# Partial logits transposed and added on VectorE, and three drains of GpSimd, in a retention and mixture-of-experts kernel

## The chip, the cores and the metric

The kernel runs on one core of one Trainium2 chip. The metric is the time of one execution in device microseconds (us), taken as the median of several runs. A core has five engines that work through their own instruction lists in order and wait for each other by semaphores: TensorE (PE, with its weight loads shown apart as PEld), VectorE (DVE), ScalarE (ACT), GpSimd (POOL) and SyncE (SP), which here only issues transfers.

## The reference

Inputs: q, k and v of 8 sequences, 8 heads, 576 positions and 64 numbers a head; 16 experts in 4 groups of 4.

```
scores = q @ k.T / 8                      # per sequence and head
x = (scores * gamma[h] ** (i - j), i >= j) @ v      # 4608 tokens x 512
g = argmax(x @ w_group);  e = argmax(x @ w_expert[g])
weight = softmax(x @ w_group)[g] * softmax(x @ w_expert[g])[e]
out = weight * (relu(x @ w1[g, e]) @ w2[g, e])      # each token by its one expert
```

All of it is float32. A token needs 20 logits: 4 for its group and 16 for the experts.

## The kernel before

The kernel has two stages. In the first (the loop at line 650) 36 tiles of 128 tokens go through the retention: products of k and q into PSUM (`pss`), a mask on VectorE (`sT`), products with v into PSUM (`px`), added products with the running state (`px` again, from `st`), and a multiplication on VectorE that makes the transposed tokens `xT` (line 640). Three tiles form a group, and each group is routed once:

- `logits` (line 351): the 512 numbers of a token lie in 4 chunks of 128. For each chunk one product gives 20 partial logits (padded to 32 rows) for the 384 tokens of the group, and the four chunks land in the four quarters of the 128 partitions of one PSUM tile, `plt`. ScalarE copies it to `lt`.
- `gate` (line 361): three products, one for each tile, of `lt` with the constant 0/1 matrix `sel`, which turns the tile (tokens onto partitions) and adds the four partial sums in one step, into `pl`, 20 numbers for each token and tile. VectorE then takes maxima (`mx`), differences (`df`) and one-hot choices (`oh`, `ob`).
- `weigh` and `places` (lines 403 and 420): the weights `wt`, and by products with triangular and all-ones matrices (`pp`) the row of each token in a table `xs` in HBM, sorted by expert. `xnat` (line 331) turns the tokens back (`pxt`, 4 transposes on TensorE for a tile), scales them (`xt`) and scatters them to `xs` with an indirect transfer of GpSimd.

`gate` of a group runs three tiles after the group's last one, between the scores of that tile and the value products of the tile before it. In the second stage (line 897) the 16 experts are worked through one after another, each in 8 steps of the hidden size, with float32 split into two halves (`wh`, `wl`; `xTh`, `xTl`), which makes three products of each one. GpSimd scatters the finished outputs of expert p - 1 during expert p (`ystore`, line 840), two blocks a step from the second step on, each paced by a one-element copy (`pace`, line 952) that waits for that step's first layer. The last group's `gate` stands in this stage, in the second step of the first expert (line 914).

The order of each engine's list is the order in which the code is written: every instruction is pinned behind the one before it on its engine (line 95). The value products of a tile write the one buffer of `px`, so they wait until VectorE has read the tile before into `xT`. On VectorE that `xT` stands behind the whole of `gate`. Helper calls all go through line 118, so rows of the profile carry that line and are told apart by the tiles' names.

Of the kernel before, what the change touches and what calls it, by code (L numbers as in the profile page):

```python
# [7 lines left out]
F32 = mybir.dt.float32  # L8
# [4 lines left out]
ALU = mybir.AluOpType  # L13
AX = mybir.AxisListType

P = 128
RG = 3
B, H, S, D = 8, 8, 576, 64
N, DM = B * S, H * D
G, EG, F = 4, 4, 1024  # L20
E = G * EG
NP = H // 2
NKC = DM // P
NFC = F // P
# [30 lines left out]
KC_BLK = KC_ROOM + 1  # L55
KC_CAP = KC_BLK + OVB
KC_CAPB = KC_CAP + E
KC_SEL = KC_CAPB + E
KC = KC_SEL + G + E

KC_MASK = KC
KC_GQ = KC_MASK + 2 * P
KC_ALL = KC_GQ + 5 * NP * P
GE = G + E
# [3 lines left out]
def moe_retention(ctx, tc, qk, kv, wgt, w1, w2, c_f, out):  # L68
# [10 lines left out]
    cf = cp.tile([P, KC], F32, name="cf")  # L79
    gk = cf[:, KC_GK : KC_GK + 5 * H].rearrange("p (c h) -> p c h", c=5)  # L80
    ident = cf[:, KC_ID : KC_ID + P]
    eid = cf[:, KC_EID : KC_EID + E]
    sel = cf[:, KC_SEL : KC_SEL + GE]
    rank = cf[:, KC_4 : KC_4 + 4]
    slb = cf[:, KC_SLB : KC_SLB + NB]
    sln = cf[:, KC_SLN : KC_SLN + 3]
# [20 lines left out]
    class Ordered:  # L107
# [15 lines left out]
    pe, dve, act, pool, sp = [  # L123
        Ordered(e_) for e_ in (nc.tensor, nc.vector, nc.scalar, nc.gpsimd, nc.sync)
    ]
# [150 lines left out]
    def ids(p):  # L276

        ii = gp.tile([P, NB], I32, name=f"ii_{p}", tag="ii", bufs=3)
        if natural(p):
            nt = len(ttiles(p))  # L280
            dve.tensor_scalar(
                ii[:, 0:nt], idns[p][:, 0:nt, 0].bitcast(I32), 2, None, ALU.logical_shift_right
            )
            dve.tensor_tensor(ii[:, 0:nt], ii[:, 0:nt], (mi0 if p == 0 else mil)[:, 0:nt], ALU.bitwise_or)
        else:
            nb = nblocks(p)
            dve.tensor_tensor(
                ii[:, 0:nb], xg[p][:, 0:nb, DQ].bitcast(I32), mia[:, p, 0:nb], ALU.bitwise_or
            )
        iis[p] = ii  # L290
# [3 lines left out]
    tiles = []  # L294
    for bp in range(B // 2):
        for j in range(9):
            if j < 8:
                b, c = 2 * bp + j // 4, j % 4
# [26 lines left out]
    sm = ctx.enter_context(tc.tile_pool(name="sm", bufs=2))  # L325
# [34 lines left out]

    def gate(t):

        pl = ps_sm.tile([P, RG, GE], F32, name=f"pl_{t}", tag="sm")
        for x_ in range(RG):
            pe.matmul(pl[:, x_, :], tiles[t]["lt"][:, x_, :], sel, start=True, stop=True)

        def t_(nm, shape, dt=F32):
            return sm.tile([P, RG] + shape, dt, name=f"{nm}_{t}", tag=nm)

        K = G + 1  # L370
        n = RG
        lv = pl.rearrange("p r (k e) -> p r k e", e=4)
        mx = t_("mx", [K])
        dve.tensor_reduce(mx, lv, AX.X, ALU.max)
        df = t_("df", [K, 4])
        dve.tensor_tensor(df, lv, mx.unsqueeze(3).to_broadcast([P, n, K, 4]), ALU.subtract)
        ex = t_("ex", [K, 4])
        act.activation(ex, df, AF.Exp)
        oh = t_("oh", [K, 4])
        dve.scalar_tensor_tensor(  # L380
            oh.rearrange("p r k e -> p (r k) e"), df.rearrange("p r k e -> p (r k) e"), 0.0,
            rank.unsqueeze(1).to_broadcast([P, n * K, 4]), ALU.is_ge, ALU.mult,
        )
        m2 = t_("m2", [K])
        dve.tensor_reduce(m2, oh, AX.X, ALU.max)
        dve.tensor_tensor(
            oh, oh, m2.unsqueeze(3).to_broadcast([P, n, K, 4]), ALU.is_equal
        )
        tiles[t]["rt"] = ex, oh
        ob = obs[-1][:, 1:, :]  # L390
        dve.tensor_tensor(
            ob.rearrange("p r (g e) -> p r g e", g=G), oh[:, :, 1:, :],
            oh[:, :, 0, :].unsqueeze(3).to_broadcast([P, n, G, EG]), ALU.mult,
        )
# [99 lines left out]
    with ExitStack() as ac:  # L494
# [155 lines left out]
        for t in range(NT + 1):  # L650
# [12 lines left out]
            r = t - PICK  # L663
# [233 lines left out]
    for p in range(E):  # L897
        for f in range(NFC):
            pc = p * NPIECE + f // 2
            if p == 0:  # L900
                new = {2: (4, 5), 3: (6,), 5: (7,)}.get(f, ())
            else:
                new = range(pc + 3, pc + 5) if f % 2 == 0 else ()
            for i in new:
                if i not in raws and (i >= len(pieces) or pieces[i][0] in ereg):
                    load_piece(i)
            layer1(p, f)
            if (p, f) == (0, 0):
                logits(NT - 1)
                xnat(NT - 5)  # L910
                pick(1)
            if (p, f) == (0, 1):
                expert_of(1)
                gate(NT - 1)
                xnat(NT - 4)
            if (p, f) == (0, 2):
                places(NT - 1)
                weigh(NT - 1)
                xnat(NT - 3)
            if (p, f) == (0, 3):  # L920
                xnat(NT - 1)
                xload(1)
            if (p, f) == (0, 4):
                for kc in range(NKC):
                    xsplit(0, kc)
            if (p, f) == (0, 6):
                for i in range(3):
                    xturn(1, i, 3)
                for kc in range(NKC):
                    xsplit(1, kc)  # L930
            if 2 * pc + f % 2 + 3 >= WHOLE:
                split(2 * pc + f % 2 + 3)
            if prev is not None:
                layer2(*prev)
                if f == 0:
                    for i in range(NKC if p > 1 else 2):
                        yturn(p - 1, i) if p > 1 else finish(0, i)
            if (p, f) == (0, 2):
                tiles_counted()
                xnat(NT - 2)  # L940
                count_experts()
            if (p, f) in ((0, 4), (0, 5)):
                next(ranks, None)
            if (p, f) == (0, 6):
                expert_of(2)
            if (p, f) == (0, 7):
                next(ranks, None)
            if p > 1 and f > 0:
                for b in range(2 * (f - 1), 2 * f):
                    if b < nblocks(p - 1):  # L950

                        pool.tensor_copy(pace, hts[p, f][0][0:1, 0:1].bitcast(F32))
                    ystore(p - 1, b)
            if f == (4 if p > 0 else 7) and p + 2 <= E:
                xpad(p + 2)
            if f == (5 if p > 0 else 7):
                xload(p + 2)
            if (p, f) == (2, NFC - 3):
                ov = overflow_places(cp)
                ovt = overflow_tables(*ov, mp, ring, cnt, cf, req, dve)  # L960
            if p in (2, 3):
                next(ovt, None) if (p, f) >= (2, NFC - 3) else None
            if f == NFC - 3 and p:
                for i in range(3):
                    xturn(p + 1, i, 3)
            if f == NFC - 2 and p:
                for kc in range(NKC):
                    xsplit(p + 1, kc)
            if f == NFC - 1 and p + 1 < E:
                ids(p + 1)  # L970
            prev = (p, f)
    for pc in range(NPIECE):
        last1(pc)
# [197 lines left out]
def _consts():  # L1171
    import numpy as np

    gamma = 1.0 - 2.0 ** (-5.0 - np.arange(H, dtype=np.float64))
    p = np.arange(P)
    c = np.zeros((P, KC_ALL), np.float32)
    pos = np.stack([ci * P + (p if ci < 4 else p % 64) for ci in range(5)])
    for ci in range(5):
        c[:, KC_GK + ci * H : KC_GK + (ci + 1) * H] = gamma[None, :] ** -pos[ci][:, None].astype(np.float64)
    c[:, KC_ID : KC_ID + P] = np.eye(P)  # L1180

    rel = p[None, :] - p[:, None]
    c[:, KC_MASK : KC_MASK + P] = rel >= 0
    c[:, KC_MASK + P : KC_GQ] = (rel >= 0) & (p[None, :] // 64 == p[:, None] // 64)

    for ci in range(5):
        for o in range(2):
            for s in range(2):
                col = KC_GQ + ((ci * 2 + o) * 2 + s) * P
                for g in range(2):  # L1190
                    c[g * D : g * D + D, col : col + P] = gamma[4 * s + 2 * g + o] ** pos[ci][None, :] / np.sqrt(D)
    c[:, KC_UP : KC_UP + P] = p[:, None] < p[None, :]
    c[:, KC_EID : KC_EID + E] = np.arange(E)

    c[:, KC_ENS : KC_ENS + E] = np.arange(E) * np.where(p < NS // 32 - P, 64, 32)[:, None]
    c[:, KC_SEL : KC_SEL + GE] = p[:, None] % 32 == np.arange(GE)
    c[:, KC_4 : KC_4 + 4] = [4, 3, 2, 1]
    c[:, KC_TRI:KC_SLB] = np.tril(np.ones((E, E))).reshape(-1)
    c[:, KC_BLK:KC_CAP] = np.arange(OVB)
    c[:, KC_CAP : KC_CAP + E] = CAPS  # L1200
    c[:, KC_CAPB : KC_CAPB + E] = -(-np.array(CAPS) // 32) * 32
    c[:, KC_SLB:KC_SLN] = np.arange(NB)[None, :] * 32 + p[:, None] % 32
    c[:, KC_SLN:KC_ROOM] = np.arange(3)[None, :] * P + p[:, None]
    c[:, KC_ROOM] = EARLY - 2 * p
    return c
# [61 lines left out]
```

## Time and profile before

| | |
|---|---|
| median of 3 runs | 620.37 us (620.37 to 621.72) |
| the profiled execution | 622.87 us, span 621.1 us |
| TensorE busy | 598.5 us, 96% of the span |
| VectorE busy | 422.0 us, 68% |
| ScalarE busy | 329.0 us, 53% |
| GpSimd busy | 263.2 us, 42% |
| mean granted TensorE clock | 0.987 |

The span runs from the first instruction to the last, and the execution's own time is 1.8 us longer. Busy shares are means over both stages. The retention fills the first 160 us or so, the experts the rest.

### The profile page before, as it was taken

The page shows a single profiled execution, that of the slowest core. Times are in us where ns is not written, and L with a number is a line of the kernel's source. Part 1 is how long each engine was busy: PE and PEld are TensorE (multiplying, and loading weights), DVE is VectorE, ACT ScalarE, POOL GpSimd, SP SyncE. Part 2 cuts the span into 40 slices and gives each one's busy share as a digit, 9 for nine tenths or more (in the row PEclk, how much of TensorE's full clock was granted, in tenths as well). Part 3 has the DMA queues.
Part 4 walks back from the last instruction along what each step waited for, and adds up shares of the span by engine and source line. Part 5 has one row for each costly group of instructions (what it writes and reads, how often), then busy time and mean ns, then how long its engine had stood idle before and what let it go on. Part 6 is the DMA issues. An engine that isn't in the chain of part 4 may idle for free.

```text
span 621.1 us, 15503 instructions
## 1 busy us (share of the span) xinstructions
PE 598.5 (96%) x5651; PEld 560.4 (90%) x5651; DVE 422.0 (68%) x955; ACT 329.0 (53%) x849; POOL 263.2 (42%) x389
## 2 busy tenths in 40 slices
PE   7899999999999999999999999999999999999990
PEld 7788788888768999999999999999999999999980
DVE  2576666677568576997767685776867768668670
ACT  3777777776255344434535353554545545546460
POOL 0022222223222017494645538185383553743751
PEclk8899999999999999999999999999999999999996
DMA  8998898877883971919375573918649467494800
GB/s 332 417 402 311 327 339 295 302 283 225 272 271 109 309 270 45 321 33 321 103 280 148 221 244 129 322 58 314 204 165 319 114 259 229 151 323 138 338 27 18
DMA packets 63262, 144.22 MB, mean 232 GB/s; under 512 B 9393, under 2 KB 30393, under 8 KB 63184
## 3 DMA queue, kind: packets, MB, share of 16 engines
q1 hardware_dynamic: 53648, 122.65, 56.8%
q0 software_dynamic: 9248, 20.35, 9.1%
q8 instruction: 45, 0.74, 0.5%
q14 instruction: 33, 0.27, 0.1%
q10 hardware_dynamic: 288, 0.22, 0.1%
HBM read 122.85 MB, written 24.88 MB: 238 GB/s over the span
## 4 chain that ended last, share of the span: by engine, by line
PE 88%; DMA 4%; DVE 2%; issue 1%; ACT 1%; POOL 1%; SPq 0%; POOLq 0%; ACTq 0%
PE py L118 33%; PE ph L118 32%; PE px L118 8%; PE pss L118 6%; PE pxt L118 3%; PE pst L118 2%; DMA b<-in_kv 2%; PE plt L118 1%; PE pl L118 1%; DMA xb<-xs 1%; POOL out L118 1%; DMA xs<-xt,sl 1%; PE phn L118 0%; PE pp L118 0%; DVE wl L118 0%
## 5 line engine op out<-in xcount | busy, mean ns | idle before, releaser
L118 POOL DMA_INDIRECT out<-y,ii x152 | 167.8, 1104 | 53.9 <-issue 37.5
L118 DVE TENSOR_TENSOR wl<-r,wh 128x512 fp32r<-128x512 f32 x260 | 167.7, 687 | 6.8 <-ACT xt L118 3.1
L118 ACT ACTIVATE hh<-ph 128x356 fp32r<-128x356 f32 (+16 forms) x128 | 53.8, 420 | 210.3 <-PE ph L118 139.9
L118 PE MATMUL ph<-xTh_m,wh 128*128 128x356 f32 (+15 forms) x488 | 147.5, 302 | 0.8 <-ACT xTh_m L118 0.8
L118 PE MATMUL ph<-xTl_m,wh 128*128 128x356 f32 (+15 forms) x488 | 146.8, 301 | 0.1
L118 ACT CAST wh<-r 128x512 fp32r<-128x512 f32 x260 | 146.9, 617 | 0.0
L118 PE MATMUL ph<-xTh_m,wl 128*128 128x356 f32 (+15 forms) x488 | 146.7, 301 | 0.0
L118 PE MATMUL py<-hh,wh 128*128 128x288 f32 (+17 forms) x480 | 145.0, 302 | 0.0
L118 PE MATMUL py<-hl,wh 128*128 128x356 f32 (+14 forms) x480 | 144.7, 302 | 0.0
L118 PE MATMUL py<-hh,wl 128*128 128x356 f32 (+14 forms) x480 | 144.6, 301 | 0.0
L118 DVE SCALAR_TENSOR_TENSOR hl<-ph,hh 128x356 fp32r<-128x356 f32 (+15 forms) x122 | 56.7, 465 | 103.7 <-ACT hh L118 71.9
L118 PEld LDWEIGHTS ph<-xTh_m,wh 128*128 128x128 f32 x488 | 92.0, 189 | 1.7 <-ACT xTh_m L118 1.2
L118 PEld LDWEIGHTS ph<-xTl_m,wh 128*128 128x128 f32 x488 | 92.1, 189 | 0.9 <-DVE xTl_m L118 0.4
L118 POOL COPY pace<-hh 1x1 f32<-1x1 f32 x140 | 34.6, 247 | 136.1 <-ACT hh L118 133.6
L118 PEld LDWEIGHTS ph<-xTh_m,wl 128*128 128x128 f32 x488 | 92.2, 189 | 0.0
L118 PEld LDWEIGHTS py<-hh,wh 128*128 128x128 f32 x480 | 90.6, 189 | 0.2
L118 POOL DMA_INDIRECT xs<-xt,sl x36 | 35.9, 996 | 129.5 <-ACT xt L118 98.6
L118 PEld LDWEIGHTS py<-hl,wh 128*128 128x128 f32 x480 | 90.4, 188 | 0.2 <-DVE hl L118 0.2
L118 PEld LDWEIGHTS py<-hh,wl 128*128 128x128 f32 x480 | 90.5, 188 | 0.0
L118 ACT ACTIVATE vs<-b,cf 128x64 f32<-128x64 f32 x288 | 72.5, 336 | 10.5 <-DMA b<-in_kv 10.5
L118 DVE TENSOR_TENSOR sT<-pss,masks 128x512 f32<-128x512 f32 x72 | 46.4, 685 | 43.8 <-PE pss L118 38.3
L118 PEld LDWEIGHTS pss<-a 64*128 64x128 f32 x576 | 36.2, 193 | 11.5 <-issue 4.6
(160 smaller groups left out, 630.5 us busy)
## 6 DMA issues: line engine op xcount, KB each, us to landing
r<-in_w SPq DMA_DIRECT2D x138, 512.0 KB
a<-in_qk SPq DMA_DIRECT2D x35, 512.0 KB
b<-in_kv SPq DMA_DIRECT2D x35, 512.0 KB
xb<-xs SPq DMA_DIRECT2D x24, 148.5 KB
xb<-xs SPq DMA_DIRECT2D x20, 165.0 KB
out<-y,ii POOLq DMA_INDIRECT x152
xb<-xs SPq DMA_DIRECT2D x12, 181.5 KB
gq<-c_f SPq DMA_DIRECT2D x5, 256.0 KB
```

Of the source, the lines that this page charges most:

```text
L118: i_ = f(*a, **k)
```

## The change

Three things are edited. In `gate` the three products with `sel` become three transposes on TensorE, each against the identity, which put all 128 rows of partial sums of a tile onto the free axis of `pl` (now 128 numbers for each token and tile instead of 20). A new reduction on VectorE adds the four numbers that belong together, which lie 32 apart, into a tile `lg` in SBUF, and the maxima and differences are taken from `lg`. The constant `sel` is gone, which makes the constants 20 columns narrower. And GpSimd gets a drain instruction, without a semaphore, at the end of the last step of experts p = 5, 10 and 14.

```diff
-    sel = cf[:, KC_SEL : KC_SEL + GE]
...
-        pl = ps_sm.tile([P, RG, GE], F32, name=f"pl_{t}", tag="sm")
+        pl = ps_sm.tile([P, RG, P], F32, name=f"pl_{t}", tag="sm")
         for x_ in range(RG):
-            pe.matmul(pl[:, x_, :], tiles[t]["lt"][:, x_, :], sel, start=True, stop=True)
+            pe.transpose(pl[:, x_, :], tiles[t]["lt"][:, x_, :], ident)
...
-        lv = pl.rearrange("p r (k e) -> p r k e", e=4)
+        lg = t_("lg", [GE])
+        dve.tensor_reduce(
+            lg, pl.rearrange("p r (a g) -> p r g a", a=NKC)[:, :, 0:GE], AX.X, ALU.add
+        )
+        lv = lg.rearrange("p r (k e) -> p r k e", e=4)
         mx = t_("mx", [K])
         dve.tensor_reduce(mx, lv, AX.X, ALU.max)
...
             if f == NFC - 1 and p + 1 < E:
                 ids(p + 1)
+            if f == NFC - 1 and p in (5, 10, 14):
+
+                pool.drain(fusable=False)
```

On VectorE, the fifth `gate` of the program stands before so, between the masks of a tile and the `xT` of the tile before it:

```order
L118 TENSOR_TENSOR sT_1404<-pss_0_1394,masks 128x512
L118 TENSOR_TENSOR sT_1404<-pss_1_1395,masks 128x512
L118 TENSOR_REDUCE mx_1411<-pl_1407 128x15
L118 TENSOR_TENSOR df_1413<-pl_1407,mx_1411 128x60
L118 SCALAR_TENSOR_TENSOR oh_1417<-df_1413,cf 128x60
L118 TENSOR_REDUCE m_14_1419<-oh_1417 128x15
L118 TENSOR_TENSOR oh_1417<-oh_1417,m_14_1419 128x60
L118 TENSOR_TENSOR ob_1267<-oh_1417 128x48
L118 TENSOR_TENSOR xT_1363<-px_1423,gq_115 128x4x128
```

After the change the same place has one reduction more, ahead of the maxima (the listing's line numbers are two lower):

```order
L116 TENSOR_TENSOR sT_1412<-pss_0_1402,masks 128x512
L116 TENSOR_TENSOR sT_1412<-pss_1_1403,masks 128x512
L116 TENSOR_REDUCE lg_1419<-pl_1415 128x60
L116 TENSOR_REDUCE mx_1421<-lg_1419 128x15
L116 TENSOR_TENSOR df_1423<-lg_1419,mx_1421 128x60
L116 SCALAR_TENSOR_TENSOR oh_1427<-df_1423,cf 128x60
L116 TENSOR_REDUCE m_14_1429<-oh_1427 128x15
L116 TENSOR_TENSOR oh_1427<-oh_1427,m_14_1429 128x60
L116 TENSOR_TENSOR ob_1275<-oh_1427 128x48
L116 TENSOR_TENSOR xT_1371<-px_1433,gq_115 128x4x128
```

The `xT` now stands behind seven instructions of the gate instead of six, and `mx` and `df` read `lg` instead of `pl`. This is so in each of the twelve gates.

On TensorE, around the seventh gate, before:

```order
L118 MATMUL pss_1_1867<-a_1383 128x128
L118 MATMUL pl_1879<-cf,lt_1853 128x20 x3
L118 MATMUL px_1895<-sT_1802,vs_1697 64x128 x8
L118 MATMUL pst_1816<-vs_1783,b_1432 64x64 x8
L118 MATMUL pxt_1917<-cf,xT_1363 128x128 x4
```

And after:

```order
L116 MATMUL pss_1_1879<-a_1391 128x128
L116 MATMUL pl_1891<-cf,lt_1865 128x128 x3
L116 MATMUL px_1909<-sT_1814,vs_1709 64x128 x8
L116 MATMUL pst_1828<-vs_1795,b_1442 64x64 x8
L116 MATMUL pxt_1931<-cf,xT_1371 128x128 x4
```

Nothing moves on TensorE. The three instructions on `pl` now have the form of those on `pxt`, which are transposes too. The lists of ScalarE, GpSimd (the drains aside) and SyncE are as before, but for the narrower transfer of the constants.

## Rows read from the trace of the kernel before

**Rows 1.** Busy time by engine in a stretch of either stage; us.

```profile
core 0: us, PE busy (x) PEld busy (x) DVE busy (x) ACT busy (x) POOL busy (x), PEclk, DMA share, GB/s
72.00:84.00 12.00, 12.00 (x199) 9.73 (x191) 7.72 (x21) 9.08 (x31) 3.26 (x5) 1.00 0.88 291
225.00:240.00 15.00, 15.00 (x97) 15.00 (x97) 8.97 (x17) 5.82 (x13) 7.66 (x13) 1.00 0.27 104
```

**Rows 2.** The chain that ended last: start us, us, what.

```profile
78.42 0.78 PE pl L118 x6
80.81 0.59 PE pxt L118 x4
...
182.69 5.17 DMA xb<-xs
```

**Rows 3.** Tile pl: ns min/median/max, first and last start us, forms.

```profile
L118 PEld LDWEIGHTS pl<-cf,lt x72: 186/192/192, 28.8 to 165.5; 128*128 128x128 f32 x72
L118 PE MATMUL pl<-cf,lt x72: 183/266/287, 28.8 to 165.5; 128*128 128x20 f32 x72
```

**Rows 4.** Tile pxt, the same columns.

```profile
L118 PEld LDWEIGHTS pxt<-cf,xT x144: 137/140/224, 34.5 to 174.8; 128*128 128x128 f32 x144
```

**Rows 5.** Timeline of weight loads around the twelfth gate: start us, us, what.

```profile
164.80 0.85 PEld L118 LDWEIGHTS pl<-cf,lt 128*128 128x128 f32 x6
165.49 0.50 PEld L118 LDWEIGHTS pxt<-cf,xT 128*128 128x128 f32 x4
```

**Rows 6.** Reductions on VectorE by form: busy us, mean ns, idle before.

```profile
L118 DVE TENSOR_REDUCE ov_bt<-ov_small 128x49 f32<-128x784 f32 x3 | 2.9, 972 | 0.1
...
L118 DVE TENSOR_REDUCE ov_cape<-ov_b 128x16 f32<-128x256 f32 x1 | 0.6, 603 | 0.0
...
L118 DVE TENSOR_REDUCE rk<-kk 128x16 f32<-128x256 f32 x1 | 0.4, 420 | 0.0
```

**Rows 7.** Timeline of VectorE in the fifth gate, the same columns.

```profile
79.65 0.21 DVE L118 TENSOR_REDUCE mx<-pl 128x15 f32<-128x60 f32 x1
79.89 0.22 DVE L118 TENSOR_TENSOR df<-pl,mx 128x60 f32<-128x60 f32 x1
...
81.03 0.69 DVE L118 TENSOR_TENSOR xT<-px,gq 128x512 f32<-128x512 f32 x1
```

**Rows 8.** The same, the xT behind gates one, four, six, ten and eleven.

```profile
31.47 0.68 DVE L118 TENSOR_TENSOR xT<-px,gq 128x512 f32<-128x512 f32 x1
...
68.56 0.68 DVE L118 TENSOR_TENSOR xT<-px,gq 128x512 f32<-128x512 f32 x1
...
93.53 0.69 DVE L118 TENSOR_TENSOR xT<-px,gq 128x512 f32<-128x512 f32 x1 [0.23 <-PE px L118]
...
144.71 0.68 DVE L118 TENSOR_TENSOR xT<-px,gq 128x512 f32<-128x512 f32 x1
...
156.66 0.68 DVE L118 TENSOR_TENSOR xT<-px,gq 128x512 f32<-128x512 f32 x1
```

**Rows 9.** Weight loads of the value products that wait for those xT.

```profile
32.37 0.85 PEld L118 LDWEIGHTS px<-sT,vs 128*64 128x64 f32 x16
...
70.03 0.85 PEld L118 LDWEIGHTS px<-sT,vs 128*64 128x64 f32 x16
...
82.65 0.85 PEld L118 LDWEIGHTS px<-sT,vs 128*64 128x64 f32 x16
...
95.30 0.85 PEld L118 LDWEIGHTS px<-sT,vs 128*64 128x64 f32 x16
...
145.66 0.85 PEld L118 LDWEIGHTS px<-sT,vs 128*64 128x64 f32 x16
...
157.39 0.85 PEld L118 LDWEIGHTS px<-sT,vs 128*64 128x64 f32 x16 [0.61 <-DVE xT L118]
```

**Rows 10.** VectorE behind the twelfth gate.

```profile
169.84 0.21 DVE L118 TENSOR_TENSOR pr<-pp,ob 128x48 f32<-128x48 f32 x1 [2.58 <-PE pp L118]
```

**Rows 11.** GpSimd in the gap where the first drain falls.

```profile
344.77 0.18 POOL L118 COPY pace<-hh 1x1 f32<-1x1 f32 x1 [7.79 <-ACT hh L118]
```

More of the change, by code (lines that the diff above doesn't have):

```diff
@@ L57 @@
 KC_CAPB = KC_CAP + E
-KC_SEL = KC_CAPB + E
-KC = KC_SEL + G + E
+KC = KC_CAPB + E
 KC_MASK = KC
@@ L1195, in _consts @@
     c[:, KC_ENS : KC_ENS + E] = np.arange(E) * np.where(p < NS // 32 - P, 64, 32)[:, None]
-    c[:, KC_SEL : KC_SEL + GE] = p[:, None] % 32 == np.arange(GE)
     c[:, KC_4 : KC_4 + 4] = [4, 3, 2, 1]
```

## Prediction

> **What bounds the kernel now.** I read the busy shares first, then the same by stretches, then the chain of waits, and last the timelines of VectorE and of TensorE's weight loads around the gates. In the stretches TensorE is busy for the whole of both shown, at a granted clock of 1.00, in the retention as among the experts [rows 1]; VectorE has a third of its time free there. The chain runs from TensorE instruction to TensorE instruction through the retention, and the three products of a gate are a link of it with 0.78 us [rows 2]. So time taken from TensorE in a gate is time taken from the program, for as long as VectorE, which the change loads more, doesn't become the one that is waited for. That is where the numbers are decided, gate by gate.
>
> **The change part by part.**
>
> *TensorE.* The products on `pl` are 72 passes for 36 instructions, 6 a gate, each with a weight load of 192 ns [rows 3]. The new instructions have the form of those on `pxt`, which are 144 for 36 tiles of four, one pass each, with a load of 140 ns [rows 4]. Four of them take 0.59 us on the chain [rows 2], so three take 0.44 us and a gate saves 0.78 - 0.44 = 0.34 us. Bounds: if the 0.59 us were a fixed cost of a group whatever its size, the saving is 0.19 us; if three take three quarters of the 0.50 us in which the four loads go out at another place [rows 5], 0.37 us, it is 0.41 us. I take 0.34 us, from the nearest row.
>
> *VectorE.* Added is one reduction of 240 numbers to 60, in PSUM, the four terms of a sum 32 numbers apart. A dense reduction costs (972 - 420) / (784 - 256) = 1.045 ns for each number and 152 ns besides, by `ov_bt` and `rk` [rows 6]. `ov_cape` reduces as many numbers as `rk`, but 16 apart, and takes 603 ns where `rk` takes 420 ns: 0.71 ns more for each number [rows 6]. No row of before reads PSUM with a step. If it costs as a dense read, the reduction takes 152 + 240 x 1.045 = 403 ns; with the step's price in SBUF, 403 + 240 x 0.71 = 574 ns; with twice that price, 744 ns. Instructions of a gate follow each other 0.03 us after the end of the one before (0.21 us of `mx`, the next 0.24 us later [rows 7]). So the `xT` behind a gate starts later by L = 0.43, 0.60 or 0.77 us. I take 0.60, which has the nearest row, and keep the others for the range. What `mx` and `df` gain by reading SBUF is under 0.01 us in rows of like size, nothing.
>
> On this cost two pages of the Trainium skill speak against each other. [Rows 6] show that a step between the numbers raises a reduction in SBUF from 420 to 603 ns. "VectorE: DVE Perf Modes", section "Mode 1× (REGULAR) — the baseline", says that one result a cycle is kept with odd strides and with PSUM operands; by that L is 0.43 us. "SBUF — State Buffer", section "Door 1: The DMA port swizzle (why `[64,N]` ≈ `[32,N]`)", says that SBUF is read in lines of 16 bytes and PSUM in lines of 8 and that each new line is paid for; by that every one of the 240 numbers pays, and L is 0.60 us or more. The trace agrees with the second as far as SBUF goes; of a stepped read of PSUM no run here has a row yet.
>
> *Gate by gate.* The value products of the next tile wait for the `xT` behind the gate, since both use the one buffer of `px`. Where VectorE was the later one, TensorE's first value product starts 0.05 us after `xT` ends (156.66 + 0.68 = 157.34, and 157.39 [rows 8, 9]). What is left between them elsewhere is slack: `xT` may come later by that much, and TensorE earlier by 0.34 us, before VectorE decides. A gate then changes the time by the larger of -0.34 and L - slack:
>
> - First gate: 31.47 + 0.68 = 32.15, product at 32.37 [rows 8, 9]; less 0.05, slack 0.17. 0.60 - 0.17 = +0.43 us.
> - Fourth, and the seventh, which has the same shape: 69.24 and 70.03 [rows 8, 9], slack 0.74. -0.14 us each.
> - Fifth, and the second and eighth like it: 81.72 and 82.65 [rows 7, 9], slack 0.88. -0.28 us each.
> - Sixth, and the third and ninth like it: 94.22 and 95.30 [rows 8, 9], slack 1.03, and VectorE has 0.23 us of waiting for TensorE ahead of this `xT` besides. The full -0.34 us each.
> - Tenth, where three small instructions on the counts stand between gate and `xT`: 145.39 and 145.66 [rows 8, 9], slack 0.22. +0.38 us.
> - Eleventh: TensorE has already waited for VectorE, 0.61 us [rows 9]; slack nothing, and what TensorE saves only lengthens its wait. +0.60 us.
> - Twelfth, among the first expert's steps: TensorE goes from the gate's products to the transposes in 0.69 us (164.80 to 165.49 [rows 5]), so three transposes save some 0.3 us, and VectorE has waited 2.58 us for TensorE before its next instruction [rows 10], which covers L. -0.30 us.
>
> Sum: 0.43 - 0.28 - 0.84 - 1.02 + 0.38 + 0.60 - 0.30 = -1.03 us. Behind the twelfth gate nothing is added or taken. The last scatters, the 5.17 us load of the second expert's tokens [rows 2] and the experts' full TensorE [rows 1] follow on from it and begin as much earlier.
>
> *Drains.* Each stands on GpSimd behind the last scatter of an expert's outputs, with no wait of its own, and ahead of the first `pace` of the next expert. Before that `pace` GpSimd stands idle for 7.79 us until ScalarE delivers `hh` [rows 11], in the shortest of the three gaps. Nothing else is queued between. The trace of before shows no drain in the middle of work; whatever it waits for, it costs nothing as long as it ends within 7.8 us. Without that cover GpSimd would pass its lateness to the scatters of `ystore`, which nobody waits for until the end, and after the third drain GpSimd has a whole expert to make up for it. Cost 0; and no gain, since no instruction on GpSimd starts earlier by it.
>
> *Constants.* Twenty columns less in one early transfer, behind which no engine waits: 0.
>
> The profiled execution took 622.87 us, 1.8 us above its span and 2.5 us above the median. The sum is a difference within it, and I put it to the median: 620.37 - 1.03 = 619.3 us.
>
> **Rivals.**
>
> *PSUM is read with a step as fast as without.* L is 0.43: first gate +0.26, fourth and seventh -0.31 each, fifth and its like -0.34 each, sixth and its like -0.34 each, tenth +0.21, eleventh +0.43, twelfth -0.30. Sum -2.1 us, 618.3 us. For it: VectorE reads PSUM in this kernel as fast as SBUF where both are dense. Against it: the step cost time in the only row that has one in float32. This is the rival that the page on VectorE named above would have.
>
> *VectorE takes over.* With L above the slack in most gates VectorE sets the pace of every gate. The gain is gone at L of about 0.73 us; at 0.77 us the sum is +0.3 us (620.7 us), and from there eight gates pay for each further 0.1 us. At L = 1.0 the same sum is +0.83 + 0.52 + 0.36 - 1.02 + 0.78 + 1.0 - 0.30 = +2.2 us, 622.5 us. It is slower by more than the bound below from L = 0.96 us, a reduction of 0.93 us, or 3.2 ns for each number read. For it: PSUM with a step is unmeasured here. Against it: `ov_cape` has 603 ns / 256 = 2.4 ns in all, its fixed part included.
>
> *TensorE saves less.* If a group of transposes costs 0.59 us whatever its size, the sum with L = 0.60 is +0.43 - 0.28 - 0.57 - 0.57 + 0.38 + 0.60 - 0.19 = -0.2 us, 620.2 us.
>
> *The drain isn't hidden.* It would have to hold GpSimd for more than the gap and then reach the transfers that fetch an expert's tokens, an expert ahead. I give it no chance of its own.
>
> **How the numbers follow.** A median here can be told from another at about 0.3%, 1.9 us: 618.5 and 622.2 us are the bounds. The forecast (L of 0.5 to 0.75, sum between -1.6 and +0.2): 0.48, no change. TensorE saves less: 0.10, no change. PSUM at full speed: 0.30, of which two thirds come out under 618.5 and a third within it. VectorE takes over: 0.12, of which 0.09 ends above the bound. That gives faster 0.20, same 0.71, slower 0.09; medians scatter, and I move 0.06 from the middle to faster, which lies nearer, and 0.01 to slower: 0.26, 0.64, 0.10. The range goes from 617.6 us (full speed for the step, 0.41 us saved in a gate) to 621.6 us (L = 0.9).
>
> **What would show it.** Twelve reductions `lg` of 0.55 to 0.6 us on VectorE; 36 passes on `pl` in place of 72; value products waiting for `xT` after gates one, ten and eleven, and after no other for more than a tenth; three gaps of GpSimd as long as before. It would be wrong if `lg` lies near 0.40 us or above 0.75 us, if twelve gates don't add up to the difference of the two medians, or if the experts' stage changes its own length.

## The result and the profile after

The changed kernel took 613.5 us (median of 4 runs, 612.01 to 614.6), the kernel before on the same chip 621.05 us (4 runs, 620.37 to 622.44). The ratio is 0.988, with a 95% interval from 0.986 to 0.990: faster by 7.5 us, where 1.1 us were forecast and the range ended at 617.6 us. The profiled execution of the changed kernel took 613.8 us, its span is 612.0 us.

The gates first, since the forecast was made there. Tile `pl` and its reduction (duration in ns, min/median/max; first and last start; forms), which answers [rows 3] and the unmeasured cost of `lg`:

```profile
L116 PEld LDWEIGHTS pl<-cf,lt x36: 138/140/143, 28.9 to 163.1; 128*128 128x128 f32 x36
L116 PE MATMUL pl<-cf,lt x36: 272/273/329, 28.9 to 163.2; 128*128 128x128 f32 x36
L116 DVE TENSOR_REDUCE lg<-pl x12: 396/398/407, 30.3 to 163.5; 128x60 f32<-128x240 f32 x12
```

36 passes of 140 ns stand for the 72 of 192 ns, as forecast. The reduction takes 398 ns, not 574. On the chain of waits (start us, us, what), at the fifth gate, the answer to [rows 2]:

```profile
75.45 0.59 PE pxt L116 x4
...
77.91 0.48 PE pl L116 x3
```

Three transposes take 0.48 us there, so a gate saves TensorE 0.78 - 0.48 = 0.30 us; 0.34 was forecast.

Weight loads of the value products behind gates one, ten and eleven (start us, us, what, in brackets the idle time ahead and who ended it), which answer [rows 9]:

```profile
32.81 0.85 PEld L116 LDWEIGHTS px<-sT,vs 128*64 128x64 f32 x16 [0.43 <-DVE xT L116]
...
143.60 0.85 PEld L116 LDWEIGHTS px<-sT,vs 128*64 128x64 f32 x16 [0.50 <-DVE xT L116]
...
155.78 0.85 PEld L116 LDWEIGHTS px<-sT,vs 128*64 128x64 f32 x16 [1.35 <-DVE xT L116]
```

At these three TensorE waits for VectorE, and at the eleventh 0.74 us longer than before. That is the pattern forecast; it can't make 7.5 us. Behind the twelfth gate VectorE waits for TensorE still, which answers [rows 10]:

```profile
167.51 0.21 DVE L116 TENSOR_TENSOR pr<-pp,ob 128x48 f32<-128x48 f32 x1 [2.09 <-PE pp L116]
```

The time is found at the other end. The page's row of TensorE in 40 equal slices of the span (tenths busy), of the kernel before:

```profile
PE   7899999999999999999999999999999999999990
```

and after:

```profile
PE   7899999999999999999999999999999999999994
```

TensorE is busy for less than a tenth of the last 15.5 us slice of before, and for four tenths of the last one after. GpSimd's last scatters, before (start us, us):

```profile
607.01 0.97 POOL L118 DMA_INDIRECT out<-y,ii  x1 [0.30 <-issue]
...
608.29 0.97 POOL L118 DMA_INDIRECT out<-y,ii  x1 [0.30 <-issue]
```

and after:

```profile
604.56 0.97 POOL L116 DMA_INDIRECT out<-y,ii  x1 [0.30 <-issue]
605.84 0.97 POOL L116 DMA_INDIRECT out<-y,ii  x1 [0.30 <-issue]
```

So 621.1 - 609.26 = 11.8 us lie behind the last scatter before, and 612.0 - 606.81 = 5.2 us after. Besides the landing of the last scatter, what runs there is no work of an engine but of its sequencer (the part of it that reads its list and issues; a `q` behind the engine's name): the instructions that close the program. The drains among them, before (count, ns min/median/max, first and last start):

```profile
L1263 SPq DRAIN  x3: 7/7/7, 611.8 to 620.5; - x3
L1263 POOLq DRAIN  x3: 40/103/8154, 612.1 to 620.8; - x3
L1263 ACTq DRAIN  x2: 8/8/8, 612.0 to 620.5; - x2
L1263 DVEq DRAIN  x2: 10/14/17, 612.2 to 620.6; - x2
```

and GpSimd's after:

```profile
L1267 POOLq DRAIN  x3: 46/103/1598, 609.6 to 611.7; - x3
```

GpSimd drains for 8154 ns before the program ends, the other engines for 7 to 17 ns and wait for it; after the change it drains for 1598 ns. That is 6.56 of the 6.6 us by which the end is shorter. SyncE's waits show it as well (us in total, times, longest), before:

```profile
SPq L1263 <- PEq L1263: 9.1, 2, 8.6
```

and after:

```profile
SPq L1267 <- PEq L1267: 2.5, 2, 2.0
```

The engine named, TensorE's sequencer, had drained long before (8 ns); GpSimd's drain ends last. What the end lost is found earlier, in the three drains that were added:

```profile
L116 POOLq DRAIN  x3: 6057/6541/11023, 332.0 to 560.0; - x3
```

Parts of these lie beside running work, since a sequencer goes ahead of its engine. The first starts at 332.0 us, GpSimd's last instruction ends at 334.4 us and the drain at 343.0 us, so 8.6 us of it stand alone; of the others 4.7 and 3.3 us. The first is longer than its cover of [rows 11]: the `pace` behind it comes 8.75 us after GpSimd's last instruction instead of 7.79.

```profile
343.18 0.18 POOL L116 COPY pace<-hh 1x1 f32<-1x1 f32 x1 [8.75 <-ACT wh L116]
```

Here the column of releasers misleads: the drain ended at 343.0 us, right ahead of it. Without drains, in e2 below, this `pace` starts at 341.97 us, and GpSimd is 0.25 us earlier there already ahead of it. GpSimd makes the microsecond up within the expert: from the twelfth transfer behind the drain on, only the 0.25 us are left.

The rest of the profile is as before. GpSimd's indirect transfers (mean ns each), which the experiments count, are the same 152 + 36 + 15 + 2 = 205:

```profile
L116 POOL DMA_INDIRECT out<-y,ii x152 | 167.6, 1103 | 50.4 <-issue 33.6 <-DVE hl L116 7.5 <-DVE y L116 7.4
L116 POOL DMA_INDIRECT xs<-xt,sl x36 | 35.9, 997 | 127.1 <-ACT xt L116 96.0 <-ACT lt L116 16.0 <-ACT vs L116 5.2
L116 POOL DMA_INDIRECT xs<-zero,pads x15 | 16.1, 1076 | 21.7 <-DVE el L116 17.4 <-ACT wh L116 1.8 <-ACT hh L116 1.2
L116 POOL DMA_INDIRECT xs<-zero,pad x2 | 1.9, 971 | 3.2 <-DVE pad L116 2.9 <-issue 0.3
```

In the timeline 91, 146 and 186 of them stand ahead of the three drains, and 19 behind the last.

### The profile page after: what moved, and what is told of

It reads as the page before. It is cut to its first block, busy times and chain, and to the rows that moved or that the text cites. A ratio compares the mean times of both kernels' runs of the same rounds, so it can differ in the third digit from the quotient of the medians.

```text
span 612.0 us, 15446 instructions
## 1 busy us (share of the span) xinstructions
PE 595.1 (97%) x5615; PEld 555.4 (91%) x5615; DVE 426.2 (70%) x967; ACT 328.0 (54%) x849; POOL 263.2 (43%) x389
## 4 chain that ended last, share of the span: by engine, by line
PE 90%; DVE 4%; DMA 2%; ACT 1%; POOL 1%; issue 1%; SPq 0%; ACTq 0%; POOLq 0%; DVEq 0%
PE ph L116 34%; PE py L116 34%; PE px L116 8%; PE pss L116 6%; PE pxt L116 3%; PE pst L116 2%; PE plt L116 2%; DMA b<-in_kv 1%; POOL out L116 1%; DVE wl L116 1%; DMA cf<-c_f 1%; PE pl L116 1%; PE phn L116 1%; DVE sT L116 1%; PE pp L116 0%
```

## The experiments

Theory A: a drain of GpSimd takes time for each indirect transfer issued since the drain before it (it settles them, as the texts below call it); the program ends with one; drains in the gaps between experts do most of that work beside TensorE. The rivals are in the expectations. Kernels that were timed together share the runs of the kernel before.

**e1, the drains alone**, on the kernel before:

```diff
+            if f == NFC - 1 and p in (5, 10, 14):
+                pool.drain(fusable=False)
```

> The kernel before with the three drains alone. Theory A (the drain at the program's end does work for GpSimd's scatters since the last drain; three drains in GpSimd's gaps do most of it early): last drain near 1.6 us where before has 8.15 us, time 6 to 7 us under before, about 614.5 us. Rival B (all of the gain is the gates', the drains only show up in the records): 621 us, last drain still 8 us or its shortening paid elsewhere.

614.31 us against 620.8 us, ratio 0.9896 [0.987, 0.9923]. The end drain is that of the changed kernel:

```profile
L1266 POOLq DRAIN  x3: 46/103/1598, 609.3 to 611.4; - x3
```

**e2, the gates alone**: the changed kernel without the three drains.

> The changed kernel without its three drains. Theory A: the gates alone give 2 to 2.6 us, about 618.5 us, and the last drain takes 8 us as before. Rival B: 613.5 us, as with the drains.

619.71 us, ratio 0.9978 [0.9963, 0.9993], and the end drain is the long one again:

```profile
L1264 POOLq DRAIN  x3: 40/103/8154, 609.4 to 618.1; - x3
```

The parts multiply to 0.9896 x 0.9978 = 0.9874, inside the interval of the whole. The drains give 6.5 us, the gates 1.1 to 1.4 us, where 2 to 2.6 us were expected of them.

**e3, three instructions that are no drains**, on the kernel before:

```diff
+            if f == NFC - 1 and p in (5, 10, 14):
+                pool.tensor_copy(pace, zero[0:1, 0:1])
```

> The kernel before with three one-element copies on GpSimd where the drains would stand. Theory A: nothing is done early, last drain 8 us, 621 us. Rival C (any three more instructions in GpSimd's list shift its code and so change the end): as with the drains, near 614.5 us.

620.36 us, ratio 1.0001 [0.9987, 1.0015], with this end drain:

```profile
L1265 POOLq DRAIN  x3: 40/103/8154, 609.7 to 618.4; - x3
```

Three more instructions in GpSimd's list do nothing; it takes a drain.

**e4, the third drain alone**, on the kernel before (`p == 14` in place of the three).

> The kernel before with one drain alone, the third. Theory A: the work of all scatters so far falls on it; with 8 us of gap it takes 7 to 10 us, the last drain is near 1.6 us again, 614.5 us, as with three. Rival D (a drain does a bounded part, and three are needed): last drain 3 to 6 us, 616.5 to 619 us.

614.58 us, ratio 0.9891 [0.9865, 0.9916]. The one drain, and those at the end:

```profile
L118 POOLq DRAIN  x1: 9338/9338/9338, 561.1 to 561.1; - x1
...
L1265 POOLq DRAIN  x3: 46/103/1608, 610.8 to 613.0; - x3
```

One drain late in the program does as much as three. 6.6 us of it lie behind GpSimd's last instruction, all inside the gap.

**e9, the changed kernel again, and e6, with a fourth drain** (`p in (5, 10, 14, 15)`), ahead of the last ten scatters.

> The changed kernel itself once more, as the yardstick for the runs beside it. Both theories: 613.5 us, 7 us below the kernel before, the drain at the end of the program 1.60 us.

> The changed kernel with a fourth drain, at the end of the last step of the sixteenth expert, ahead of the last ten scatters. Theory A, a drain takes about 84 ns for each transfer of GpSimd since the drain before it: the fourth takes about 0.8 us in a gap, the drain at the end 0.8 us instead of 1.60, and the program 612.8 us, 0.7 us less than the changed kernel. Rival E, what is left at the end is fixed once any drain stood before: the end drain stays at 1.60 us, and the time at 613.5 us. Rival F, the fourth drain holds the last scatters up: 613.5 us or more, with the end drain short.

e9: 613.51 us, ratio 0.9869 [0.9845, 0.9893]. e6: 612.58 us, ratio 0.9859 [0.9834, 0.9885], with this end drain:

```profile
L1267 POOLq DRAIN  x3: 46/103/863, 609.1 to 610.5; - x3
```

735 ns are gone from the end as theory A has it, and rival E falls on that row. Rival F falls on the first of the last ten scatters, which waits for VectorE's `y` and not for the drain, with the same 7.35 us of idle time ahead of it as in e9:

```profile
592.78 1.14 POOL L116 DMA_INDIRECT out<-y,ii  x1 [7.35 <-DVE y L116]
```

The fourth drain, for nine transfers, lasts 1.55 us behind GpSimd's last instruction, twice what was expected; e5 shows why. That the median lies 0.9 us below e9's agrees with theory A, but the intervals overlap, so a gain in time is not shown by the runs themselves.

**e5, a drain behind every one of the first fifteen experts**, two at the eighth:

```diff
-            if f == NFC - 1 and p in (5, 10, 14):
-                pool.drain(fusable=False)
+            if f == NFC - 1 and p + 1 < E:
+                pool.drain(fusable=False)
+                if p == 7:
+                    pool.drain(fusable=False)
```

> The changed kernel with a drain at the end of each of the first fifteen experts instead of three, and two in a row at the end of the eighth. Theory A, about 84 ns for each transfer since the last drain: the first (about 36 transfers) 3.0 us, the others (10 or 11 transfers each) 0.85 to 1.0 us, the second of the pair 0.1 us, the end drain 1.6 us (19 transfers), the time 613.5 us. Rival E, a drain among running work has a cost of its own, whatever came before it: the second of the pair and all others take 3 us or more.

612.76 us, ratio 0.9864 [0.9839, 0.9888], end drain 1598 ns. The pair at the eighth expert, and the last one:

```profile
L116 POOLq DRAIN  x2: 53/2576/5098, 383.5 to 388.6; - x2
...
L116 POOLq DRAIN  x1: 4352/4352/4352, 558.5 to 558.5; - x1
```

With nothing issued between, a drain takes 53 ns, so it has no cost of its own and rival E falls. But most sizes of theory A were wrong here. Behind GpSimd's last instruction the first drain lasts 3.3 us for 39 transfers, as expected; those of the second to sixth expert last 4.0 to 6.8 us with 13 transfers or fewer (the one of 6.8 us has 3), those of the seventh to eleventh 1.6 to 3.2 us with 11, and those of the twelfth to fifteenth 1.6 us with 10. A drain right behind a transfer also lasts until that one has landed. The last transfer ahead of the 6.8 us drain of the second expert, and of the 1.6 us drain of the fifteenth:

```profile
L116 POOL DMA_INDIRECT xs<-zero,pads x1: 972/972/972, 200.5 to 200.5; - x1
DMA to landing us min/median/max: 7.6/7.6/7.6
...
L116 POOL DMA_INDIRECT out<-y,ii x1: 985/985/985, 560.3 to 560.3; - x1
DMA to landing us min/median/max: 2.2/2.2/2.2
```

By the trace's records of single packets, each of these drains ends 0.6 to 2.1 us behind the last packet of the transfers ahead of it.

**e7, the drains behind the gap instead of ahead of it**: behind the first `pace` of experts 6, 11 and 15.

```diff
+                    if (f, b) == (1, 0) and p in (6, 11, 15):
+                        pool.drain(fusable=False)
                     ystore(p - 1, b)
```

> The changed kernel with its three drains moved behind the idle gap: behind the one-element copy that ends the gap, ahead of the first scatter of experts 6, 11 and 15. Theory A, the drain itself does the work, transfer by transfer: the drains last as long as in the changed kernel net of what was running, 8.6, 4.6 and 3.3 us, and hold the scatters behind them up; the time still 613.5 us, the end drain 1.60 us. Rival G, the transfers only have to become old enough, and the idle gap does that as well: the three drains take under 0.5 us each, the time 613.5 us.

613.87 us, ratio 0.9879 [0.9856, 0.9903].

```profile
L116 POOLq DRAIN  x3: 3537/4772/7717, 342.1 to 570.9; - x3
```

The gap of 8 us did nothing for them: rival G falls, the drain does its work itself. All had landed 3 to 8 us ahead of these drains, so the sizes are clean: 91, 55 and 40 transfers in 7717, 4772 and 3537 ns, which is (7717 - 4772) / 36 = 81.8 and (4772 - 3537) / 15 = 82.3 ns for each. (Whether the price goes by the transfer or by its rows is not told apart.) The scatters behind them start up to 7.7 us later (8.38 us of idle time where others have 0.64), and the program is as fast as e9: GpSimd had that much to spare within an expert.

**e10 and e11, where the 99 come from.** By 82 ns each, the 8154 ns of before are 99 transfers, though 205 were issued. In e4 the 6.6 us are 80 transfers, though 186 were issued: the same 106 less.

> The kernel before with one drain, at the end of the last step of the ninth expert, 124 of GpSimd's 205 transfers in. In the kernel before, the end drain's 8.15 us are (8154 - 40) / 82 = 99 transfers, so 106 had been settled on the way; 3.21 us of issue stand ahead of the 114th. Theory H, the 106 are settled together there: the drain takes 18 x 82 ns = 1.5 us, or up to 2.2 us with the landing of the last, behind GpSimd's last instruction, and the end drain, for 81 transfers, 81 x 82 + 40 = 6.7 us; the program about 1.5 us under the kernel before. Rival I, they are settled little by little, or later: this drain takes 8 to 10 us, the end drain 6.7 us all the same.

The edit of e10 missed its place: the kernel that ran was e4 once more, with the drain behind the fifteenth expert (614.41 us, end drain 1608 ns, again 6.6 us behind GpSimd's last instruction), and tells nothing of when the 106 were settled. e11 is the one meant (`p == 8` in e4).

> The kernel before with one drain, now really at the end of the last step of the ninth expert, 124 of GpSimd's 205 transfers in. Theory H, 106 transfers are settled together ahead of the 114th: the drain takes 18 x 82 ns = 1.5 us, or up to 2.2 us with the landing of the last, behind GpSimd's last instruction; the 3.21 us of issue ahead of the 114th stay; the end drain, for 81 transfers, is 81 x 82 + 40 = 6.7 us. Rival I, they are settled little by little, or later: this drain takes 8 to 10 us, the end drain 6.7 us all the same.

619.66 us, one run (before 621.68 us). The end drain is 6672 ns for 81 transfers, as expected:

```profile
L1265 POOLq DRAIN  x3: 46/103/6672, 610.3 to 617.6; - x3
```

The drain itself:

```profile
L118 POOLq DRAIN  x1: 6276/6276/6276, 414.8 to 414.8; - x1
```

4.0 us of it lie behind GpSimd's last instruction: more than theory H gives, half or less of what rival I needs. The last packet of the transfer ahead lands 2.4 us behind that instruction, and the 1.6 us left are about the size of theory H's 18 transfers (1.5 us), but at 82 ns each 4.0 us have room for 48. So at least 76 of the 124 were settled by then; in what steps is not shown.

**e12, the drain one expert earlier** (`p == 7`), right ahead of the 114th transfer.

> The kernel before with one drain, at the end of the last step of the eighth expert, 113 transfers in, right ahead of the 114th. Theory H: the drain takes 113 x 82 ns and 0.2 to 1.5 us besides, 9.5 to 10.8 us behind GpSimd's last instruction; the 3.21 us of issue ahead of the 114th shrink to the 0.6 us of other steps; the end drain, for 92 transfers, is 7.6 us, the program only 0.5 us under the kernel before. Rival I: the 3.21 us stay, since they have another cause, and the end drain is 7.6 us or less.

620.9 us, one run. The drain ends 9.3 us behind GpSimd's last instruction, 113 x 82 ns and nothing besides, a little under the 9.5 to 10.8 us expected; the end drain is

```profile
L1265 POOLq DRAIN  x3: 46/103/7570, 610.7 to 618.8; - x3
```

for 92 transfers. And the long issue ahead of the 114th is gone. Before (start us, us):

```profile
398.34 0.18 POOL L118 COPY pace<-hh 1x1 f32<-1x1 f32 x1 [9.00 <-ACT hh L118]
401.72 0.99 POOL L118 DMA_INDIRECT out<-y,ii  x1 [3.21 <-issue]
```

and in e12:

```profile
397.18 0.18 POOL L118 COPY pace<-hh 1x1 f32<-1x1 f32 x1 [9.38 <-ACT hh L118]
398.00 1.43 POOL L118 DMA_INDIRECT out<-y,ii  x1 [0.65 <-DVE wl L118]
```

That speaks for theory H: without a drain, GpSimd settles earlier transfers of itself at the 114th, hidden in the experts' stage. But the 3.21 us are only 2.56 us more than e12's 0.65, which at 82 ns have room for 31 transfers; so either the 106 were not settled all at that place, or they cost less there than in a drain. That is not shown.

**e8, the reduction from SBUF**: on the changed kernel,

```diff
+        pls = tiles[t]["lt"]
+        act.copy(pls, pl)
-            lg, pl.rearrange("p r (a g) -> p r g a", a=NKC)[:, :, 0:GE], AX.X, ALU.add
+            lg, pls.rearrange("p r (a g) -> p r g a", a=NKC)[:, :, 0:GE], AX.X, ALU.add
```

> The changed kernel, but ScalarE copies the transposed partial sums from PSUM to SBUF and the reduction lg reads them there, with the same step. Theory S, a step costs in SBUF and not in PSUM: lg takes about 574 ns instead of 398 ns (152 + 240 x 1.045 + 240 x 0.71). Rival T, the forecast's price was wrong for SBUF too: lg stays at about 400 ns. The copy stands in the way of the gate in both, so the program gets longer than the changed kernel by up to 5 us.

```profile
L116 DVE TENSOR_REDUCE lg<-lt x12: 567/571/580, 29.9 to 170.1; 128x60 f32<-128x240 f32 x12
```

571 ns from SBUF, 398 ns from PSUM, the same shape and step. Theory S holds, within 3 ns of the estimate. (620.38 us, one run, 6.9 us above the changed kernel where up to 5 us were expected: the copy costs each gate more than the step did.)

## Why the prediction was wrong

**The step that failed** is the one on the drains: "Cost 0; and no gain, since no instruction on GpSimd starts earlier by it." The cost was right: all three were covered or made up for, as it said, and 6.5 us came from the drains all the same (e1). The reason was wrong. An instruction of GpSimd's does end earlier, the drain that closes the program, and the trace of before had it: 8154 ns on GpSimd's sequencer, 8.6 us of waiting on SyncE's, and a nearly empty last slice of TensorE. The sum followed the path to the last scatter at 609.26 us and let the 11.8 us behind it stand as a constant. Nor did the drains have a rival in which they shorten the program; the only one was the one in which they aren't hidden. Two of the signs that it gave for being wrong came: `lg` near 0.40 us, and gates that don't add up to the difference of the medians.

It could have been priced from before as a bound, without knowing the mechanism. Other engines drain in 7 to 17 ns, GpSimd in 8154; so up to 8.1 us of the end may move with what GpSimd has done since its last drain. The rule measured afterwards is linear, to 10 ns, over the end drains of which the count is known, 46 ns and 81.7 for each transfer since the last: 863 ns for 10, 1598 for 19, 6672 for 81, 7570 for 92.

The Trainium skill, "VectorE: DVE Perf Modes", section "The DRAIN you can't avoid", says that the drains which open and close a program take about 12 ns on each of the five engines. The rows of the closing drains agree for SyncE, ScalarE and VectorE (7 to 17 ns) and not for GpSimd (8154 and 1598 ns); the measurement decides.

**L was mis-sized**: 0.60 us taken, 0.43 measured (398 ns and the 0.03 us between instructions). The step's price of [rows 6] is true of SBUF (571 ns in e8) and was carried to PSUM, where there is none: 398 ns against 403 for a dense read by the same rows. Of the two pages of the Trainium skill that the prediction weighed, "VectorE: DVE Perf Modes", section "Mode 1× (REGULAR) — the baseline", agrees with the rows on PSUM (398 ns) and not on SBUF (571 ns). With "SBUF — State Buffer", section "Door 1: The DMA port swizzle (why `[64,N]` ≈ `[32,N]`)", it is the other way round; what that section of the Trainium skill says of PSUM, it says of matmuls. The rival "PSUM is read with a step as fast as without" was the right one for the gates. "VectorE takes over" did not happen. (The range itself was added up a little off: by the prediction's own rule for a gate its ends are some 617.8 and 621.7 us, not 617.6 and 621.6; 613.5 us lies outside either.)

**TensorE's saving** is 0.30 us a gate, inside its bounds of 0.19 and 0.41. From the second gate to the tenth, eight intervals, the old gate in e1 (start us, us):

```profile
40.41 0.21 DVE L118 TENSOR_REDUCE mx<-pl 128x15 f32<-128x60 f32 x1
...
140.86 0.21 DVE L118 TENSOR_REDUCE mx<-pl 128x15 f32<-128x60 f32 x1
```

and the new one in e2:

```profile
42.22 0.40 DVE L116 TENSOR_REDUCE lg<-pl 128x60 f32<-128x240 f32 x1
...
140.30 0.40 DVE L116 TENSOR_REDUCE lg<-pl 128x60 f32<-128x240 f32 x1
```

That is 100.45 and 98.08 us, 2.37 / 8 = 0.30 us a gate, and none of the eight is held up by VectorE, as with L = 0.43 none should. Single profiles scatter here too: seven with the old gate have 100.45 to 100.87 us, six with the new one 98.07 to 98.88 us, which is 0.20 to 0.35 us a gate.

**The gate-by-gate account held.** With L = 0.43 it gives +0.26 at the first gate, +0.21 at the tenth and +0.43 at the eleventh. TensorE waits 0.43 and 0.50 us for VectorE at the first two, and 0.74 us longer than before at the eleventh, which is L and the 0.30 us that TensorE saved. In sum the rival's -2.1 us, or -1.8 us with 0.30 for 0.34 (eight gates and the twelfth at -0.30, and 0.90 back). e2's runs give -1.4 us with an interval from -0.4 to -2.3. The forecast's -1.03 us is also inside, so the medians alone don't tell them apart; the length of `lg` and the waits do.

**The profiles' starts differ by themselves.** VectorE's first instruction in the first gate starts at 28.18 us in e1 and at 30.25 us in the changed kernel, with little of what was edited ahead of it; TensorE's granted clock between 12 and 24 us was 1.00 and 0.86 (the mean over the levels of 1.2 and 2.4 GHz). So single executions differ by some 2 us at the start alone, and the sums above are taken between points behind that stretch.

**The experts' stage** kept its length, as forecast: from VectorE's first turn of the second expert's tokens (`xTf`) to the start of the last scatter 608.29 - 188.01 = 420.28 us before and 605.84 - 185.45 = 420.39 us after.

## What to carry to other kernels

Follow the chain to the end of the span, not to the last useful instruction: read what stands between them, sequencers included, before calling it a constant. Where GpSimd issues many indirect transfers, look at the drain that closes the program, and put a drain into the last gap in which GpSimd is idle for long enough, as late as possible; here one did as much as three (e4). Before charging a strided read, ask which memory the row came from.

## What the runs showed of the hardware

- A drain of GpSimd works through its indirect transfers since the last one at 82 ns each (e7 and the end drains), does not profit from idle time ahead of it (e7), and takes 53 ns when there is nothing to settle (e5). Right behind a transfer it lasts until that one has landed: at least 1.55 us (e6), and 6.8 us for three transfers where the landing took 7.6 us from the issue (e5).
- GpSimd also settles transfers without a drain: 3.21 us of issue ahead of the 114th in the kernel before, gone in e12, and by 82 ns each 99 left of 205 at the end and 80 of 186 in e4. How many at that point, and in what steps, stays open (e11, e12).
- Another sequencer instruction at the end follows the same count: before the closing drain GpSimd takes 2170 ns with 99 transfers open, 558 ns with 19 and 378 ns with 10 (e6). From the end of the last scatter to the closing drain it is 2.9 us before and 2.8 us after, so it hardly shows in the time.
- VectorE sums 240 numbers in fours that lie 128 bytes apart in 398 ns from PSUM (the changed kernel) and in 571 ns from SBUF (e8).
